# Decode block with its backward pass on one core: weight gradients and the x gradient as two background streams with buffers of their own

## The chip, the core and the metric

The kernel runs on one core of a Trainium2 chip. A core has a matrix engine (PE, with its weight loads PEld), a vector engine (DVE), a scalar engine (ACT), GpSimd (POOL) and SyncE (SP), each with its own in-order instruction queue. They work on SBUF tiles and on PSUM banks and wait for each other by semaphores. DMAs are issued from the queue of an engine and run beside it. The metric is the device time of one execution in microseconds, the median of several runs. A profiled execution gives the trace; its span is from the first to the last instruction.

## The reference, cut to what matters

One decode step (one position, batch 2) of a pre-norm block, and its vector-Jacobian product:

```python
B, Sq, D = 2, 1, 640;  Hq, Hkv, Sk, Dh = 32, 32, 4096, 128;  Dff = 1728
h   = x + attention(layernorm(x) @ wq, k_cache, v_cache) @ wo      # softmax over 4096 positions
out = h + relu(layernorm(h) @ w1) @ w2
_out, _vjp = jax.vjp(_f, A_x, A_k_cache, A_v_cache, A_wq, A_wo, B_w1, B_w2)
return (_out, *_vjp(grad_out))
```

The outputs are out_0 (the block's output), out_1 (gradient of x), out_2 and out_3 (gradients of the two caches, 2 x 32 x 4096 x 128 bf16, 67 MB each), and the weight gradients out_4 (wq, 640 x 4096), out_5 (wo, 4096 x 640), out_6 (w1) and out_7 (w2). With batch 2 each weight gradient is a product of rank 2: two rows of one vector set times two rows of another.

## The kernel before

**Two phases of 64 head turns.** Phase 1 (`p1_iter`, i = 0 to 65) takes one (batch, head) after the other: it loads the K and V tile (1 MB each), transposes K on PE, forms scores and softmax, and the products that later steps need. Phase 2 (`p2_iter`, j = 0 to 64) takes V again (tile W; 11 of the 64 are kept from phase 1), transposes it as pairs (`pair_transpose`, L366), gets `dp`, and writes two outer products on DVE, gK and gV (`outer_half`, L733, two halves each), which POOL stores to out_2 and out_3 (L773, L792). `plan` (L966) lays both side by side: phase 2 starts with i = 44 on every second turn, and from j = 11 it runs alone. A "turn" below is one such j. A turn without phase 1 is seven passes of the inner loop at L1060.

**The order is written by hand.** The program issues instructions in the order in which this Python code yields; no engine reorders its queue. Beside the turns, generators run in the background: `bg` (the middle layers; `go_group`, which gives the heads' output gradients goc and GQc; and last `mlp_out`, the product with w2 and out_0) and `bg2` (`fin_gen`, the weight gradients and the x gradient). `bg_step` gives each a credit per pass (its rate), and a generator pays what it yields; a yield of 0.0 means that it waits. `wait(n)` lets n counted steps go by (times `spread`, 2 when phase 2 runs alone), so that an instruction isn't put in the queue before its operand is likely to be there. After the last turn `forced` is set and what is left runs at once.

**Buffers.** Twelve equal homes ("big", 8 KB per partition) hold K, V, W, w2 and wq pieces, output tiles ot, and gK and gV. `take` and `give` hand them out from two lists, "ld" and "g"; `share(n)` moves homes to "g". `pump` issues the loads of `queue` on SP as "ld" homes come free; `reserve` (L1047) and `spare` (L1048) keep some back for `fin_gen` and `mlp_out`. A tile given back is handed out again in turn, and its new writer waits for the old reader or store.

**The weight gradients.** `rows_of` (L799) brings columns into row form: a copy on ACT (wide), four PE products into the PSUM bank "mid", a copy back. `outer_rows` (L818) forms an output group by group: up to three products of rank 2 into the banks mid, m and a, then three ACT copies to ot (L840), then a store from POOL's queue (L842). `gx_piece` (L856) loads one of six pieces of wq (wqs, L862), waits, transposes it on PE eight blocks at a time (L873, copies L875), and sums the products with GQc in bank m (L885), one add to gx1 per piece (L889). `fin_gen` runs out_7, out_6 (with a gx piece after each group), out_5 (the same), the rest of gx, the layer-norm backward and out_1 (`store_row`, L572, one buffer orow), and then out_4 with the rows of GQ. It is created when w1 is no longer needed (("w1", 1), L1049), in w1's place in SBUF.

**PSUM.** Eight banks: tps 2, sps 3, and m, a and mid one each.

Of the kernel before, what the change touches and what calls it, by code (L numbers as in the profile page):

```python
# [15 lines left out]
def kernel(  # L16
# [20 lines left out]
    nc = tc.nc  # L37
# [39 lines left out]
    homes = {"ld": list(range(NBIG)), "g": []}  # L77
    free = {"ld": NBIG, "g": 0}
    owned = {"ld": NBIG, "g": 0}
    stores = [0]  # L80
    spare = [2]
    home_of = {}

    def take(tag, shape, name):
        assert free[tag] > 0, (tag, name)
        free[tag] -= 1
        k = homes[tag].pop(0)
        t = big.tile(shape, BF16, tag=f"big{k}", bufs=1, name=name)
        home_of[id(t)] = (tag, k, t)
        return t  # L90

    def give(t, to=None):
        tag, k, _ = home_of.pop(id(t))
        to = to or tag
        owned[tag] -= 1
        owned[to] += 1
        free[to] += 1
        homes[to].append(k)

    def share(n):  # L100

        stores[0] = n
        while owned["g"] < n and free["ld"] > 0:
            homes["g"].append(homes["ld"].pop(0))
            for d in (free, owned):
                d["ld"] -= 1
                d["g"] += 1
# [464 lines left out]
    def store_row(col_bf, n, dst):  # L572
# [3 lines left out]
        r = small.tile([16, 128], BF16, tag="orow", bufs=1, name="orow")  # L576
# [49 lines left out]
    def mlp_out():  # L626
# [3 lines left out]
        for k in range(NW2):  # L630
            while free["ld"] < spare[0]:
                yield
            t = load_w2(k, "ld")
            yield from wait(8)
# [105 lines left out]
    def p2_iter(j, busy):  # L740
# [45 lines left out]
        give(c["W"], "g" if owned["g"] < stores[0] else "ld")  # L786
# [31 lines left out]
    def outer_rows(L, nrow, R, N, out_ap, cc, between=None):  # L818
# [5 lines left out]
        for c0 in range(0, cc, grp):  # L824
            gn = min(grp, cc - c0)
            while free["ld"] < spare[0]:
                yield
            ot = take("ld", [128, grp, N], "ot")
            todo = [(k, n0, min(512, N - n0)) for k in range(gn) for n0 in range(0, N, 512)]
            for t0 in range(0, len(todo), 3):  # L830
                part = []
                for k, n0, nn in todo[t0:t0 + 3]:
                    q = 32 * (fw[0] % 4)
                    o_ps = pst([128, 512], FP32, ("mid", "m", "a")[len(part)], "o_ps")
                    nc.tensor.matmul(o_ps[0:P, 0:nn], lhsT=L[q:q + B, bass.ds(c0 + k, P, step=cc)],
                                     rhs=R[q:q + B, n0:n0 + nn], start=True, stop=True)
                    part.append((o_ps, k, n0, nn))
                    fw[0] += 1
                for o_ps, k, n0, nn in part:
                    nc.scalar.copy(out=ot[0:P, k, n0:n0 + nn], in_=o_ps[0:P, 0:nn])  # L840
                yield 0.5 * len(part)
            nc.gpsimd.dma_start(out=out_v[:, c0:c0 + gn, :], in_=ot[0:P, 0:gn, :])  # L842
            give(ot)
            if between is not None:
                yield from between()

    def fin_gen(fin):
        gx1 = fin.tile([128, ND, B], FP32, tag="gx1", name="gx1")
        nc.vector.memset(gx1[:], 0.0)
# [3 lines left out]
        yield from wait(4)  # L853
        gx_next = [0]

        def gx_piece(k):  # L856

            hn = min(QP, H - k * QP)
            while free["ld"] < spare[0]:
                yield  # L860
            t = take("ld", [128, ND, QP * 128], "wqs")
            nc.sync.dma_start(out=t[:, :, 0:hn * 128], in_=wq_r[:, :, k * QP * 128:(k * QP + hn) * 128])  # L862
            yield from wait(6)
            todo = [(c, j) for j in range(hn) for c in range(ND)]
            acc = None
            prev = None
            for t0 in range(0, len(todo) + GT, GT):
                part = todo[t0:t0 + GT]
                nxt = None
                if part:  # L870
# [160 lines left out]
    for n, (i, j) in enumerate(plan):  # L1031
# [3 lines left out]
        if j == 0:  # L1035
            stores[0] = 3
# [87 lines left out]
```

## Time and profile before

| what | value |
|---|---|
| median of 6 runs | 1010.05 us (1005.01 to 1019.57) |
| the profiled execution | 1010.56 us; span 1008.8 us; mean granted TensorE clock 0.80 |
| busy in the span | PE 787.1, PEld 694.5, DVE 657.7, ACT 586.5, POOL 107.5 us |
| moved | 363.25 MB, mean 360 GB/s |
| ot copies (L840) | 160, the first at 698.9, the last at 1001.3 us |
| wqs transposes (L873) | 160, from 777.6 to 944.3 us |
| wqs issue to landing | 24.8 / 28.1 / 31.5 us (min, median, max) |
| ot issue to landing | 4.1 / 6.2 / 19.6 us |
| last gK store issued | 956.96 us |

A busy time is the sum of an engine's instruction times; it says nothing of where the engine was needed. The view by windows cuts it into stretches and gives the granted clock, the share of time in which the 16 DMA engines were busy, and the rate. The view of waits lists whose idle time was ended by whom. Phase 1 runs alone to about 330 us, with phase 2 to about 525 us; then phase 2 runs alone.

### The profile page before, as it was taken

The page shows a single profiled execution, that of the slowest core. Times are in us where ns is not written, and L with a number is a line of the kernel's source. Part 1 is how long each engine was busy: PE and PEld are TensorE (multiplying, and loading weights), DVE is VectorE, ACT ScalarE, POOL GpSimd, SP SyncE. Part 2 cuts the span into 40 slices and gives each one's busy share as a digit, 9 for nine tenths or more (in the row PEclk, how much of TensorE's full clock was granted, in tenths as well). Part 3 has the DMA queues.
Part 4 walks back from the last instruction along what each step waited for, and adds up shares of the span by engine and source line. Part 5 has one row for each costly group of instructions (what it writes and reads, how often), then busy time and mean ns, then how long its engine had stood idle before and what let it go on. Part 6 is the DMA issues. An engine that isn't in the chain of part 4 may idle for free.

```text
span 1008.8 us, 30245 instructions
## 1 busy us (share of the span) xinstructions
PE 787.1 (78%) x13169; PEld 694.5 (69%) x13173; DVE 657.7 (65%) x1289; ACT 586.5 (58%) x1261; POOL 107.5 (11%) x219
## 2 busy tenths in 40 slices
PE   6999999989899989999877746468485948764846
PEld 5988898989888888888866545356364836653611
DVE  3555767755387678787878888888673736663700
ACT  4666656667667767777644434245363727553747
POOL 0000000000000010000012121112211211211201
PEclk9999999999699989999995757576555658565655
DMA  9999999994577789999999999999799998999835
GB/s 350 416 401 384 355 378 407 363 386 172 208 255 284 301 314 377 423 422 421 401 353 425 423 371 425 407 426 413 306 379 412 364 420 333 422 424 417 329 128 208
DMA packets 63205, 363.25 MB, mean 360 GB/s; under 512 B 5696, under 2 KB 20928, under 8 KB 22880
## 3 DMA queue, kind: packets, MB, share of 16 engines
q1 hardware_dynamic: 42416, 212.18, 54.1%
q0 software_dynamic: 20656, 149.14, 35.7%
q8 instruction: 103, 1.69, 0.6%
q14 instruction: 30, 0.25, 0.1%
HBM read 212.16 MB, written 149.13 MB: 358 GB/s over the span
## 4 chain that ended last, share of the span: by engine, by line
PE 42%; DMA 29%; DVE 10%; issue 10%; ACT 7%; POOL 1%; SPq 0%; POOLq 0%; DVEq 0%; ACTq 0%
PE t_ps L353 10%; PE m_ps L408 10%; DMA wqs<-in_A_wq_dram 8%; DMA out_dram<-gK 8%; DMA out_dram<-gV 8%; DMA Kt<-in_A_k_cache_dram 6%; PE t_ps L374 5%; PE m_ps L423 4%; DVE gV L735 4%; ACT t_sb L358 4%; PE s_ps L364 4%; DVE gK L735 3%; PE dp_ps L387 1%; PE t_ps L345 1%; PE t_ps L873 1%
## 5 line engine op out<-in xcount | busy, mean ns | idle before, releaser
L358 ACT COPY t_sb<-t_ps 128x1024 bf16<-128x1024 bf16 x223 | 219.5, 1014 | 54.3 <-PE t_ps L353 52.1
L379 ACT COPY t_sb<-t_ps 128x512 f32<-128x512 f32 x256 | 148.7, 589 | 111.1 <-PE t_ps L374 107.7
L408 PE MATMUL m_ps<-pk,Vt 128*128 128x129 bf16 x2048 | 201.6, 226 | 5.9 <-issue 5.9
L374 PE MATMUL t_ps<-ident_f,Wt 128*128 128x128 f32 x848 | 181.5, 360 | 2.7 <-DMA Wt<-in_A_v_cache_dram 1.3
L415 DVE TENSOR_TENSOR pk<-Kt,ep 128x2048 bf16<-128x2048 bf16 x128 | 156.0, 1219 | 25.7 <-ACT ep L465 25.7
L735 DVE TENSOR_TENSOR gK<-rb,gsp 128x2048 bf16<-128x2048 bf16 x128 | 152.2, 1228 | 31.6 <-DMA out_dram<-gV 18.1
L735 DVE TENSOR_TENSOR gV<-rb,pp 128x2048 bf16<-128x2048 bf16 x128 | 152.3, 1218 | 23.4 <-DMA out_dram<-gK 11.0
L353 PE MATMUL t_ps<-ident_bf,Kt 128*128 128x128 bf16 x2048 | 155.6, 227 | 4.5 <-issue 2.4
L408 PEld LDWEIGHTS <-Vt 128*128 128x128 bf16 x2048 | 133.4, 102 | 15.3 <-issue 10.0
L374 PEld LDWEIGHTS t_ps<-ident_f,Wt 128*128 128x128 f32 x848 | 129.1, 186 | 16.8 <-issue 6.4
L353 PEld LDWEIGHTS <-Kt 128*128 128x128 bf16 x2048 | 129.1, 102 | 8.5 <-issue 4.1
L387 PEld LDWEIGHTS <-t_sb 128*128 128x128 bf16 x2048 | 90.7, 104 | 51.0 <-ACT t_sb L379 41.1
L387 PE MATMUL dp_ps<-gom,t_sb 128*128 128x2 bf16 x2048 | 93.9, 167 | 23.7 <-ACT t_sb L379 22.6
L364 PE MATMUL s_ps<-qc,t_sb 128*128 128x1 bf16 x2048 | 89.1, 164 | 13.2 <-ACT t_sb L358 8.6
L364 PEld LDWEIGHTS <-t_sb 128*128 128x128 bf16 x2048 | 79.8, 97 | 18.2 <-ACT t_sb L358 12.8
L840 ACT CAST ot<-o_ps 128x512 bf16<-128x512 f32 (+4 forms) x160 | 65.9, 491 | 22.4 <-DMA out_dram<-ot 13.2
L792 POOL DMA_DIRECT2D out_dram<-gV x64 | 34.2, 534 | 393.1 <-DVE gV L735 288.0
L356 DVE COPY t_sb<-t_ps 128x1024 bf16<-128x1024 bf16 x33 | 22.8, 692 | 66.3 <-PE t_ps L353 66.3
L518 ACT ACTIVATE MT<-m_ps,rtot 128x128 bf16<-128x128 f32 x64 | 23.6, 368 | 70.0 <-PE m_ps L408 65.8
L423 PE MATMUL m_ps<-ep,Kt 128*128 128x1 bf16 x2048 | 61.0, 163 | 1.8 <-ACT OU L519 1.2
L773 POOL DMA_DIRECT2D out_dram<-gK x64 | 34.0, 531 | 256.6 <-DVE gK L735 221.4
L423 PEld LDWEIGHTS <-Kt 128*128 128x128 bf16 x2048 | 58.6, 96 | 2.1 <-issue 1.7
(186 smaller groups left out, 872.8 us busy)
## 6 DMA issues: line engine op xcount, KB each, us to landing
Kt<-in_A_k_cache_dram SPq DMA_DIRECT2D x64, 1024.0 KB, 9.6
Vt<-in_A_v_cache_dram SPq DMA_DIRECT2D x64, 1024.0 KB, 8.5
out_dram<-gV POOLq DMA_DIRECT2D x64, 1024.0 KB, 11.2
out_dram<-gK POOLq DMA_DIRECT2D x64, 1024.0 KB, 10.8
Wt<-in_A_v_cache_dram SPq DMA_DIRECT2D x53, 1024.0 KB, 10.7
wo_t<-in_A_wo_dram SPq DMA_DIRECT2D x4, 1280.0 KB, 11.0
out_dram<-ot POOLq DMA_DIRECT2D x5, 1024.0 KB, 4.1
wq_t<-in_A_wq_dram SPq DMA_DIRECT2D x5, 960.0 KB, 10.0
```

Source lines behind the costliest of these rows:

```text
L353: nc.tensor.transpose(t_ps[:, j, :], nat[:, g * GT + j, :], ident_bf[:])
L358: nc.scalar.copy(out=t_sb[:], in_=t_ps[:])
L364: nc.tensor.matmul(dst[:, sc:sc + 1], lhsT=t_sb[:, j, :], rhs=vec, start=True, stop=True)
L374: nc.tensor.transpose(t_ps[:, j, :], natf[:, 2 * cc:2 * cc + 2, :].rearrange("p c k -> p (c k)"), ident_f[:])
L379: nc.scalar.copy(out=t_sb[:], in_=t_ps[:])
L387: nc.tensor.matmul(dst[:, sc:sc + 2], lhsT=v[:, j, :, par], rhs=vecs[:, par, :], start=(par == 0), stop=(par == 1))
L408: nc.tensor.matmul(r["m"][:, 0:129], lhsT=r["V"][:, sc, :], rhs=r["pk"][sc // HALF][:, sc % HALF, 0:129], start=False, stop=(sc == NSC - 1))
L415: nc.vector.tensor_tensor(out=p["pk"][k][:, :, 0:128].rearrange("p s (a two) -> p s a two", two=2), in0=p["K"][:, sl, :].rearrange("p s (a ...
L423: nc.tensor.matmul(r["m"][:, 129:130], lhsT=r["K"][:, sc, :], rhs=r["ep"][:, sc, 0:1], start=(sc == 0), stop=False)
L735: nc.vector.tensor_tensor(out=pairs_view(dst[:, sl, :]), in0=row.rearrange("p (a two) -> p a two", two=2)[:, None, :, :].to_broadcast([128 ...
L792: nc.gpsimd.dma_start(out=natural(out_3, b, h), in_=gV[:])
L840: nc.scalar.copy(out=ot[0:P, k, n0:n0 + nn], in_=o_ps[0:P, 0:nn])
```

## The change

It does the following.

- Homes come in four lists: "ld", "g", "f" (tiles of the weight gradients) and "q" (w2 and wq pieces). `share` takes a wanted number for each list, and a home that is given back goes to a list that lacks one. From turn 36 the wanted numbers are ld 4, g 4, f 3, q 2; when both background streams have ended, ld 7 and g 6. `reserve` and `spare` are gone.
- A thirteenth home, `big2`, is made in w1's place beside the pool fin and goes to "f".
- `fin_gen` forms the weight gradients alone: out_7, out_6, out_5, out_4, the last two in halves of 16 heads. `gx_gen` is a third background list, `bg3`, with a rate of its own (0.45; bg2's is 0.65, it was 0.85).
- `outer_rows` puts its products in the banks m and a in turn, each followed one step later by the copy of the one before; a home rests 13 steps before it is used again (`rested`). Once all of goc is there (`late`), every third copy is on DVE. The stores are issued from ACT's queue.
- `gx_gen` fetches wq pieces as soon as all of goc is there and a "q" home is free, two at a time at most, and starts a piece 20 steps after its fetch. Its products go by column blocks to bank mid, with an add on DVE for each group of eight.
- `mlp_out` takes its w2 pieces from "q" and waits 12 steps instead of 8. `store_row` has two orow buffers.
- Steps are counted in `bg_step(1, ...)`. During phase 1 bg2 gets no credit. What is left at the end runs in rounds over bg, bg3 and bg2.

```diff
-    homes = {"ld": list(range(NBIG)), "g": []}
-    free = {"ld": NBIG, "g": 0}
-    owned = {"ld": NBIG, "g": 0}
-    stores = [0]
-    spare = [2]
+    homes = {"ld": list(range(NBIG)), "g": [], "f": [], "q": []}
+    free = {tag: len(v) for tag, v in homes.items()}
+    owned = dict(free)
+    wanted = {}
+    pools = [big] * NBIG
     home_of = {}
+    given_at = {}
     def take(tag, shape, name):
         assert free[tag] > 0, (tag, name)
         free[tag] -= 1
         k = homes[tag].pop(0)
-        t = big.tile(shape, BF16, tag=f"big{k}", bufs=1, name=name)
+        t = pools[k].tile(shape, BF16, tag=f"big{k}", bufs=1, name=name)
         home_of[id(t)] = (tag, k, t)
...
+    def goes_to(tag):
+
+        if owned[tag] > wanted.get(tag, NBIG):
+            for other in homes:
+                if owned[other] < wanted.get(other, 0):
+                    return other
+        return tag
+
     def give(t, to=None):
         tag, k, _ = home_of.pop(id(t))
-        to = to or tag
+        to = to or goes_to(tag)
         owned[tag] -= 1
         owned[to] += 1
         free[to] += 1
         homes[to].append(k)
-
-    def share(n):
-
-        stores[0] = n
-        while owned["g"] < n and free["ld"] > 0:
-            homes["g"].append(homes["ld"].pop(0))
-            for d in (free, owned):
-                d["ld"] -= 1
-                d["g"] += 1
+        given_at[k] = step[0]
+
+    def rested(tag, n):
+
+        return free[tag] > 0 and (forced[0] or step[0] >= given_at.get(homes[tag][0], -n) + n)
+
+    def share(**want):
+
+        wanted.clear()
+        wanted.update(want)
+        for tag in homes:
+            while free[tag] > 0 and goes_to(tag) != tag:
+                to = goes_to(tag)
+                homes[to].append(homes[tag].pop(0))
+                for d in (free, owned):
+                    d[tag] -= 1
+                    d[to] += 1
+
+    def more_home(tag, pool):
+        homes[tag].append(len(pools))
+        pools.append(pool)
+        free[tag] += 1
+        owned[tag] += 1
...
-        r = small.tile([16, 128], BF16, tag="orow", bufs=1, name="orow")
+        r = small.tile([16, 128], BF16, tag="orow", bufs=2, name="orow")
...
-            while free["ld"] < spare[0]:
+            while free["q"] < 1:
                 yield
-            t = load_w2(k, "ld")
-            yield from wait(8)
+            t = load_w2(k, "q")
+            yield from wait(12)
...
-        give(c["W"], "g" if owned["g"] < stores[0] else "ld")
+        give(c["W"], "g" if j < H and owned["g"] < 3 else None)
...
-    def outer_rows(L, nrow, R, N, out_ap, cc, between=None):
+    late = [False]
+
+    def outer_rows(L, nrow, R, N, out_ap, cc):
         P = nrow // cc
...
         out_v = out_ap.rearrange("(p c) n -> p c n", c=cc)
         for c0 in range(0, cc, grp):
             gn = min(grp, cc - c0)
-            while free["ld"] < spare[0]:
-                yield
-            ot = take("ld", [128, grp, N], "ot")
+            while not rested("f", 13):
+                yield 0.0
+            ot = take("f", [128, grp, N], "ot")
             todo = [(k, n0, min(512, N - n0)) for k in range(gn) for n0 in range(0, N, 512)]
-            for t0 in range(0, len(todo), 3):
-                part = []
-                for k, n0, nn in todo[t0:t0 + 3]:
+            made = []
+            for x in range(len(todo) + 1):
+                if x < len(todo):
+                    k, n0, nn = todo[x]
                     q = 32 * (fw[0] % 4)
-                    o_ps = pst([128, 512], FP32, ("mid", "m", "a")[len(part)], "o_ps")
+                    o_ps = pst([128, 512], FP32, "ma"[fw[0] % 2], "o_ps")
+                    fw[0] += 1
                     nc.tensor.matmul(o_ps[0:P, 0:nn], lhsT=L[q:q + B, bass.ds(c0 + k, P, step=cc)],
                                      rhs=R[q:q + B, n0:n0 + nn], start=True, stop=True)
-                    part.append((o_ps, k, n0, nn))
-                    fw[0] += 1
-                for o_ps, k, n0, nn in part:
-                    nc.scalar.copy(out=ot[0:P, k, n0:n0 + nn], in_=o_ps[0:P, 0:nn])
-                yield 0.5 * len(part)
-            nc.gpsimd.dma_start(out=out_v[:, c0:c0 + gn, :], in_=ot[0:P, 0:gn, :])
+                    made.append((o_ps, k, n0, nn))
+                    yield 0.3
+                if x > 0:
+                    o_ps, k, n0, nn = made[x - 1]
+                    if late[0] and x % 3 == 0 and x < len(todo):
+                        nc.vector.tensor_copy(out=ot[0:P, k, n0:n0 + nn], in_=o_ps[0:P, 0:nn])
+                    else:
+                        nc.scalar.copy(out=ot[0:P, k, n0:n0 + nn], in_=o_ps[0:P, 0:nn])
+                    yield 0.3
+            nc.scalar.dma_start(out=out_v[:, c0:c0 + gn, :], in_=ot[0:P, 0:gn, :])
             give(ot)
-            if between is not None:
-                yield from between()
     def fin_gen(fin):
-        gx1 = fin.tile([128, ND, B], FP32, tag="gx1", name="gx1")
-        nc.vector.memset(gx1[:], 0.0)
         FIN["wide"] = [fin.tile([128, 4, 4, 32], BF16, tag="wide", bufs=2, name="wide") for _ in range(2)]
         for w in FIN["wide"]:
             nc.vector.memset(w[:], 0.0)
-        yield from wait(4)
-        gx_next = [0]
-
-        def gx_piece(k):
-
+        yield from wait(2)
...
+        yield from outer_rows(FIN["ar"], Dff, FIN["gr"], D, out_7, Dff // 96)
+        yield from rows_of(fin, ghfc, NF, "ghfr", "rX")
+        yield from rows_of(fin, x2c, ND, "x2r", "rD")
+        yield from outer_rows(FIN["x2r"], D, FIN["ghfr"], Dff, out_6, ND)
+        HH = H // 2
+        while ("gh1", B - 1) not in done:
+            yield
+        yield from rows_of(fin, gh1c, ND, "gh1r", "rD")
+        for s0 in range(0, H, HH):
+            yield from rows_of(fin, OFc[:, s0:s0 + HH, :], HH, "OFr", "rX")
+            yield from outer_rows(FIN["OFr"], HH * 128, FIN["gh1r"], D, out_5[s0 * 128:(s0 + HH) * 128, :], HH)
+        yield from rows_of(fin, x1c, ND, "x1r", "rD")
+        for s0 in range(0, H, HH):
+            while not all(("go", B - 1, h) in done for h in range(s0, s0 + HH)):
+                yield
+            yield from rows_of(fin, GQc[:, s0:s0 + HH, :], HH, "GQr", "rX")
+            yield from outer_rows(FIN["x1r"], D, FIN["GQr"], HH * 128, out_4[:, s0 * 128:(s0 + HH) * 128], ND)
+
+    def gx_gen(fin):
+        gx1 = fin.tile([128, ND, B], FP32, tag="gx1", name="gx1")
+        nc.vector.memset(gx1[:], 0.0)
+        tiles = []
+
+        def fetch():
+            while len(tiles) < NQ and free["q"] > 0:
+                k = len(tiles)
+                hn = min(QP, H - k * QP)
+                t = take("q", [128, ND, QP * 128], "wqs")
+                nc.sync.dma_start(out=t[:, :, 0:hn * 128], in_=wq_r[:, :, k * QP * 128:(k * QP + hn) * 128])
+                tiles.append((t, step[0]))
+
+        while not all(("go", B - 1, h) in done for h in range(H)):
+            yield 0.0
+        for k in range(NQ):
+            while k >= len(tiles) or (step[0] < tiles[k][1] + 20 and not forced[0]):
+                fetch()
+                yield 0.0
+            t = tiles[k][0]
             hn = min(QP, H - k * QP)
-            while free["ld"] < spare[0]:
-                yield
-            t = take("ld", [128, ND, QP * 128], "wqs")
-            nc.sync.dma_start(out=t[:, :, 0:hn * 128], in_=wq_r[:, :, k * QP * 128:(k * QP + hn) * 128])
-            yield from wait(6)
-            todo = [(c, j) for j in range(hn) for c in range(ND)]
-            acc = None
+            todo = [(c, j) for c in range(ND) for j in range(hn)]
             prev = None
             for t0 in range(0, len(todo) + GT, GT):
                 part = todo[t0:t0 + GT]
...
                     nxt = (t_sb, part)
                     if t0 + GT >= len(todo):
                         give(t)
+                        fetch()
                     yield 0.9
                 if prev is not None:
-                    if acc is None:
-                        acc = pst([128, ND, B], FP32, "m", "gx_ps")
+                    acc = pst([128, ND, B], FP32, "mid", "gx_ps")
+                    c0, c1 = prev[1][0][0], prev[1][-1][0] + 1
                     for x, (c, j) in enumerate(prev[1]):
-
                         nc.tensor.matmul(acc[:, c, :], lhsT=prev[0][:, x, :], rhs=GQc[:, k * QP + j, :],
-                                         start=(c == 0 and j == 0), stop=(c == ND - 1 and j == hn - 1))
+                                         start=(x == 0 or prev[1][x - 1][0] != c),
+                                         stop=(x == len(prev[1]) - 1 or prev[1][x + 1][0] != c))
+                    nc.vector.tensor_tensor(out=gx1[:, c0:c1, :], in0=gx1[:, c0:c1, :], in1=acc[:, c0:c1, :], op=ALU.add)
                     yield
                 prev = nxt
-            nc.vector.tensor_tensor(out=gx1[:], in0=gx1[:], in1=acc[:], op=ALU.add)
-
-        def gx_ready():
-
-            k = gx_next[0]
-            if k < NQ and all(("go", B - 1, h) in done for h in range(k * QP, min(H, (k + 1) * QP))):
-                gx_next[0] += 1
-                yield from gx_piece(k)
-
-        yield from rows_of(fin, acol, NF, "ar", "rF")
-        yield from rows_of(fin, gc, ND, "gr", "rD")
-        yield from outer_rows(FIN["ar"], Dff, FIN["gr"], D, out_7, Dff // 96)
-        yield from rows_of(fin, ghfc, NF, "ghfr", "rF")
-        yield from rows_of(fin, x2c, ND, "x2r", "rD")
-        yield from outer_rows(FIN["x2r"], D, FIN["ghfr"], Dff, out_6, ND, gx_ready)
-        while ("gh1", B - 1) not in done:
-            yield
-        yield from rows_of(fin, OFc, H, "OFr", "rH")
-        yield from rows_of(fin, gh1c, ND, "gh1r", "rD")
-        yield from outer_rows(FIN["OFr"], HD, FIN["gh1r"], D, out_5, HD // 128, gx_ready)
-        while gx_next[0] < NQ:
-            yield from gx_ready()
-            yield
...
+            yield from wait(2)
...
-        yield from rows_of(fin, GQc, H, "GQr", "rH")
-        yield from rows_of(fin, x1c, ND, "x1r", "rD")
-        yield from outer_rows(FIN["x1r"], D, FIN["GQr"], HD, out_4, ND)
...
-        q = (bg, bg2)[k]
+        step[0] += int(k == 1)
+        q = (bg, bg2, bg3)[k]
         credit[k] = min(credit[k] + rate, 2.0) if q else 0.0
         while q and credit[k] > 0.0:
...
-    RATE2 = 0.85
+    RATE2 = 0.65
+    RATE3 = 0.45
...
-        if j == 0:
-            stores[0] = 3
         if i is None and plan[n - 1][0] is not None:
-            share(4)
-        if j == H + KEPT[1]:
-            share(5)
+            share(ld=KEPT[1] + 3, g=4)
+        if fin is not None and not bg2 and not bg3:
+            share(ld=7, g=6)
+        elif fin is not None and j >= H + KEPT[1] - 1:
+            share(ld=4, g=4, f=3, q=2)
         if j is not None:
             while g2 is not None:
                 p2_step()
             if j < NP1:
                 bg_until(("go", *turns[j]))
...
-        reserve[0] = 2 if bg2 and j is not None and j >= H + 4 else 0
-        spare[0] = 1 if j is not None and j >= H + 2 else 2
         if i is None and ("w1", 1) in done and fin is None:
             wts.release()
             fin = tc.alloc_tile_pool(name="fin", bufs=1)
+            big2 = tc.alloc_tile_pool(name="big2", bufs=1)
+            more_home("f", big2)
             bg2.append(("fin", fin_gen(fin)))
+            bg3.append(("gx", gx_gen(fin)))
+        late[0] = all(("go", B - 1, h) in done for h in range(H))
...
+                bg_step(2, RATE3)
...
     forced[0] = True
     slot[0] = 99
-    while bg2:
-        bg_one(bg2)
+    left = [q for q in (bg, bg3, bg2) if q]
+    while left:
+        for q in left:
+            bg_one(q)
+        left = [q for q in left if q]
+    big2.release()
```

More of the change, by code (lines that the diff above doesn't have):

```diff
@@ new lines, in fin_gen @@
+        yield from rows_of(fin, acol, NF, "ar", "rX")
+        yield from rows_of(fin, gc, ND, "gr", "rD")
+        yield from outer_rows(FIN["ar"], Dff, FIN["gr"], D, out_7, Dff // 96)
[6 more added lines that the diff above has]
+        yield from rows_of(fin, gh1c, ND, "gh1r", "rD")
@@ L918, in fin_gen @@
             nc.vector.tensor_copy(out=gxo[:], in_=gx_bf[:, :, b])
+            yield from wait(2)
             store_row(gxo[:], ND, out_1[b].rearrange("s (c p) -> (s c) p", p=128))
             yield
-        yield from rows_of(fin, GQc, H, "GQr", "rH")
-        yield from rows_of(fin, x1c, ND, "x1r", "rD")
-        yield from outer_rows(FIN["x1r"], D, FIN["GQr"], HD, out_4, ND)
     bg = []
     bg2 = []
+    bg3 = []
     done = set()
-    credit = [0.0, 0.0]
+    credit = [0.0, 0.0, 0.0]
     def bg_one(q):
@@ L945, in bg_step @@
     def bg_step(k, rate):
-        step[0] += k
-        q = (bg, bg2)[k]
+        step[0] += int(k == 1)
+        q = (bg, bg2, bg3)[k]
         credit[k] = min(credit[k] + rate, 2.0) if q else 0.0
@@ L995 @@
     queue.insert(0, ("wq", 0))
-    reserve = [0]
     def pump():
@@ L1004, in pump @@
                 tag = "ld"
-                if free["ld"] <= reserve[0]:
+                if free["ld"] < 1:
                     return
@@ L1017 @@
     pump()
-    fin = None
+    fin = big2 = None
     g2 = None
@@ L1084 @@
             bg_step(0, rate)
-            bg_step(1, RATE2)
+            bg_step(1, 0.0)
         if i is not None and i in (H + 1, NP1 + 1):
```

## The prediction, made before the run

> **What bounds the kernel now.** I read the page's slices first, then the busy time and DMA rate by stage, then the same view over the places where the rate drops, then the waits, then the timeline of the end.
>
> ```profile
> PEclk9999999999699989999995757576555658565655
> DMA  9999999994577789999999999999799998999835
> HBM read 212.16 MB, written 149.13 MB: 358 GB/s over the span
> ```
>
> By stage, a line's fields are the window, its length, busy time (instructions) of PE, PEld, DVE, ACT and POOL, then granted clock, DMA share and GB/s:
>
> ```profile
> 525.00:592.00 67.00, 39.80 (x501) 35.05 (x502) 55.92 (x94) 24.85 (x47) 12.73 (x26) 0.64 1.01 419
> 592.00:710.00 118.00, 73.18 (x861) 61.98 (x860) 103.59 (x172) 50.58 (x106) 22.50 (x46) 0.66 1.00 407
> 710.00:745.00 35.00, 21.91 (x197) 17.59 (x196) 24.19 (x41) 18.03 (x46) 7.27 (x15) 0.50 0.84 316
> 745.00:955.00 210.00, 145.07 (x1672) 118.57 (x1671) 118.22 (x140) 113.37 (x232) 39.49 (x76) 0.63 0.97 395
> 955.00:1008.80 53.80, 29.09 (x94) 9.33 (x93) 3.81 (x16) 31.98 (x76) 4.78 (x9) 0.50 0.40 163
> ...
> 720.00:730.00 10.00, 8.23 (x66) 5.88 (x66) 5.24 (x9) 7.66 (x20) 1.05 (x2) 0.50 0.52 201
> 780.00:790.00 10.00, 9.76 (x125) 7.87 (x122) 6.23 (x9) 7.95 (x16) 1.58 (x3) 0.67 0.76 272
> 835.00:845.00 10.00, 9.38 (x137) 8.19 (x135) 8.21 (x11) 8.49 (x16) 2.26 (x4) 0.73 0.65 214
> 935.00:940.00 5.00, 4.46 (x49) 4.03 (x49) 3.84 (x5) 2.98 (x8) 1.83 (x4) 0.50 0.56 226
> ```
>
> From 525 us on the transfers set the pace: 419 GB/s, share 1.01, no engine full but DVE. The rate fails in three kinds of place: around 720, in short holes between 780 and 940, and from 955 to the end, where 53.8 us move 163 GB/s.
>
> The waits (who, for whom: us in total, times, longest):
>
> ```profile
> PE t_ps L873 <- DMA wqs<-in_A_wq_dram: 45.9, 4, 17.8
> DVE orow L577 <- DMA out_dram<-orow: 21.6, 2, 17.5
> PE o_ps L835 <- ACT ot L840: 18.7, 12, 13.6
> ACT ot L840 <- DMA out_dram<-ot: 13.2, 1, 13.2
> ```
>
> The timeline of POOL at the end, with the idle time before each issue in brackets:
>
> ```profile
> 985.50 0.53 POOL L842 DMA_DIRECT2D out_dram<-ot  x1 [24.43 <-ACT ot L840]
> 989.70 0.53 POOL L842 DMA_DIRECT2D out_dram<-ot  x1 [3.66 <-ACT ot L840]
> 1002.27 0.53 POOL L842 DMA_DIRECT2D out_dram<-ot  x1 [3.66 <-ACT ot L840]
> ```
>
> Each hole follows one engine standing in order: ACT 13.2 us at 707 (a store tile given out again before its store had landed), PE 11.8 us at 766 and again until 920 (the wq piece not landed), DVE 17.5 us at 819 (one orow buffer). During each stall the DMA stays full from its backlog; the hole comes afterwards. In the end stretch nothing overlaps: the last gK leaves at 957.0, then x gradient, rows of GQ and all of out_4 in a row.
>
> **The change, part by part.** The sum stands against the profiled run: span 1008.8, run 1010.56 us; the median, 1010.05, lies 0.5 lower. Bytes are unchanged. From 525 they are 178.9 MB (rates times windows, in 25 us steps); the full rate is taken as 421 GB/s, as most full 5 us windows read 419 to 429.
>
> Here a rule speaks against any gain. The windows above hold 419 over 67 us. The Trainium skill, "DMA: Bandwidth & Descriptors", Specifications, gives about 358 GB/s as the HBM limit of a core and says that side binds HBM-to-SBUF traffic. By it 361.3 MB need 1009 us, exactly the span, and overlapping the end could win nothing. By the row, 421 is held for long stretches and 358 is only a mean over full and empty ones. I follow the row.
>
> 1. *The end (out_4 and x gradient into the streams).* 53.8 us x 163 GB/s = 8.77 MB, at 421 20.8 us: 33.0 us go. A last transfer stays: an ot store lands 6.2 us after issue (median), 2.5 of that being 1 MB at 421, so 4 us come back. This needs the streams to finish in time. A turn without phase 1 makes seven background steps. The f stream adds 0.65 per step; rows cost 1.7 per four columns, a part 0.6, and with one home a tile rests 13 steps. Counted through all six row/product blocks that is about 270 steps, 38 turns. It can begin at turn 21 (w1 done at 590, gV20 issued at 589.5), so it ends near turn 60 of 64. The gx stream begins when all of goc is there (743, turn 40); a piece costs 5.6 at 0.45, or the 20-step age, about 16 steps: six pieces, some 95 steps, to turn 54. The three w2 pieces can be held off by gx's immediate refetch of both q homes; then 3 x 24 steps plus little, to turn 62 or 63. Cover: the turns themselves. If w2 misses it, some 10 us return.
>
> 2. *ot's reuse (rest of 13 steps, three f homes).* The hole 720-730 is worth 10 x (1 - 201/421) = 5.2 us. It goes. The rest of 710-745 (8.7 in all) I leave, since four freed W homes now pass to f and q in turn.
>
> 3. *Earlier wq, 20 steps of age, two homes; orow bufs 2.* Holes at 780, 835 and 935: 3.5 + 4.9 + 2.3 = 10.7 us go if the stalls before them go.
>
> Gross: 33.0 - 4 + 5.2 + 10.7 = 44.9.
>
> 4. *What it adds.* Matmuls, row matmuls (112), transposes (160) and copies (160) stay the same in number. Stores rise from 17 to 18 and move from POOL to ACT. The trace shows no ACT issue; unblocked SP issues take 0.33 to 0.70 us, so 18 x 0.38 = 7 us of ACT (bounds 0 and 12.6), with t_sb and rb copies queued behind, for which PE waits. ACT is 54% busy in 745-955: nothing on the path. POOL loses L842's waits, so gK and gV stores never stand behind ACT. SP keeps the same wqs and w2 issues, in order among W loads that wait for freed homes.
>
> PE gets new waits. The gx sums now go to DVE in 21 adds instead of 6 (15 x 0.162 = 2.4 us of DVE), each holding the single mid bank until DVE has passed its outer products, 2.36 us a pair; rows, w2 sums and the next gx group queue behind it on PE. A late copy on DVE (every third part from turn 40 on: 16 of out_5, 10 of out_4) holds m or a likewise. With half a pair each, and 0.4 for the copy, 15 x 1.2 + 26 x 1.6 = 60 us of PE order; bounds 0 and twice that. How much of a PE stall reaches the DMA? In the trace some 80 us (45.9 + 18.7 + 17.5) left 15.9 us of holes, a fifth. So 12 us (0 to 24).
>
> Last, does a wq piece land in 20 steps? A turn of 7.5 to 8.7 us makes that 21 to 25 us; the six rows read 24.8 to 31.5, median 28.1, with W running up to four ahead. Now W has four homes, three ahead: 28.1 x 4/5 = 22.5, no stall. Against it: the same page, Queues, rings and completion order, says each DMA engine goes round-robin over the queue rows with work. The trace has one row of loads and one of stores; ot on ACT makes a third, so loads fall from a half to a third while an ot store is in flight: 34 us, 11 short, six times 66 us of PE, a fifth is 13 us. Eighteen stores of 6 to 10 us fill some 40% of 340 us, so I take 4 us.
>
> Sum: 44.9 - 12 - 4 = 28.9; span 980, time 981.7, against the median 981.
>
> **Rivals.**
> *A, the DMA runs full to the end.* 525 + 178.9/0.421 + 4 = 954, time 956. For: 420 was held even while PE stood. Against: three streams now meet in the same turns.
> *C, the gain is given back as a PE bound.* At the half clock (0.50 in most rows) a turn's own work is 16 W transposes x 0.27 + their products and rb 2.2 = 6.5 us; over turns 36 to 60 that is 156 us, and parts 43, gx 25.5, rows 13 come on it: 238 us, 9.9 a turn, over the DMA's 8.7. With a quarter of step 4's waits unhidden, 253. Then 710 + 9 (out_7 and part of out_6, 3.7 MB, moved ahead of it) + 253 + 4 turns x 7.4 + 8 = 1010 with the last landing, time 1012. Against: at 840-860 PE is dense, its clock 0.93 to 1.0, and a transpose takes 0.16.
> *D, slower.* The mid bank: PE cold as in C, and every one of the 21 adds finds DVE at the start of a pair: 238 + 21 x 2.4 = 288 us, time 1046. It decides from 24 us of such waits unhidden on a cold PE (10.9 us a turn). For: PE waited up to 1.4 us for a gx add already. Against: DVE was idle over 40% of 745-955.
> *E, the early start fails.* If the home in w1's place serves nothing before turn 38, when the first W home has been handed over and has rested, 26 turns x 7 x 0.65 = 118 of the 140 units of rows and parts are done; 22, or 37 parts at 0.5 us, stand at the end: 18 us, time 995.
>
> **How the numbers follow.** Likeliest (981, own range 966 to 996) 0.50; A 0.20; C 0.11; D 0.13; E 0.06, half of it within 1%. A measurement of this kernel can tell about 1% from no change. Faster 0.20 + 0.50 + 0.03 = 0.73; within 1% 0.11 + 0.03 = 0.14; slower 0.13. The range 954 to 1014 leaves out D and the edge of A.
>
> **What would show it.** Right: ot copies from about 605 instead of 698.9; 400 GB/s or more until within 15 us of the end; no GQ rows after the last gK; no orow wait; the stall at wqs under 5 us each; turns 40 to 60 of 8.7 to 9.3 us. Wrong: PE full at clock 0.5 with DMA under 0.9; PE or DVE waits on mid's adds above 40 us; a last gK after 985; w2 or out_0 after it.

## The result, and the profile after

The changed kernel takes 1000.11 us (median of 33 runs, 992.26 to 1014.44), the kernel before 1009.85 us in the same comparison (70 runs): ratio 0.991, 95% interval 0.9892 to 0.9928. (The ratio leaves out runs that are over 1.5% slower than the fastest of their kernel, so it is not quite that of the medians.) The gain is real, and a third of the 29 us that were forecast. The profiled execution has a span of 1000.9 us at a mean granted clock of 0.777 (before 1008.8 us, 0.800).

The page, slices of 25.0 us:

```profile
PEclk9999998999799989999996756555655555655657
DMA  9999999995577789999999999998998999998878
HBM read 212.16 MB, written 149.13 MB: 361 GB/s over the span
```

The two poor slices at the end are now 7 and 8 instead of 3 and 5, and slice 29 (700 us) is a 9 instead of a 7; in exchange slices at 675, 750 and 900 us have fallen from 9 to 8. The view by windows says where (window, length, busy us and instructions of PE, PEld, DVE, ACT, POOL, granted clock, DMA share, GB/s):

```profile
525.00:592.00 67.00, 38.50 (x486) 33.89 (x485) 56.20 (x97) 24.77 (x47) 13.35 (x26) 0.64 1.01 423
592.00:710.00 118.00, 85.82 (x761) 68.28 (x761) 89.99 (x150) 57.34 (x131) 18.73 (x41) 0.53 0.95 372
710.00:745.00 35.00, 27.36 (x269) 21.20 (x268) 28.74 (x46) 20.14 (x44) 7.27 (x15) 0.60 0.98 393
745.00:955.00 210.00, 166.50 (x1541) 123.11 (x1539) 116.18 (x169) 112.82 (x231) 28.30 (x59) 0.54 0.93 366
955.00:1000.90 45.90, 23.41 (x267) 18.12 (x266) 29.24 (x39) 15.84 (x30) 9.10 (x17) 0.69 0.85 343
```

Read as time lost against the 421 GB/s of the prediction, length x (1 - rate / 421):

| stretch | before | after | best version (below) |
|---|---|---|---|
| 592-710 | 3.9 us | 13.7 us | 8.7 us |
| 710-745 | 8.7 | 2.3 | 2.2 |
| 745-955 | 13.0 | 27.4 | 7.0 |
| 955 to the end | 33.0 | 8.5 | 4.9 |
| sum | 58.6 | 52.0 | 22.8 |

The end and the stretch around the hole at 720 gained 31 us, nearly the forecast (33.0 - 4 + 5.2 = 34). The two long stretches in the middle lost 24 us more than before, while PE was busy for 73% and 79% of them. The waits from 592 to 970 us (who, for whom: us in total, times, longest; "issue" is standing that no wait explains):

```profile
DVE gx L945 <- PE gx_ps L942: 48.1, 20, 5.7
PE o_ps L862 <- ACT ot L871: 47.0, 56, 2.7
PEld L862 <- issue: 35.2, 52, 3.0
PEld t_ps L397 <- issue: 28.9, 32, 2.0
PE rw_ps L833 <- DVE gom L304: 10.1, 1, 10.1
```

The waits of before for orow and for wqs are not in this list (PE waits 0.3 us for orow, and no longer for wqs). In their place PE, about to make a product of rank 2 (o_ps, L862), stands 56 times for the ACT copy out of the bank that it needs (L871). The timeline at 630 us shows how (start, duration, engine, line, operation, idle time before it in brackets):

```profile
630.16 0.26 PEld L862 LDWEIGHTS <-ar 2*96 2x96 bf16 x3 [0.33 <-issue]
630.16 0.76 PE L862 MATMUL o_ps<-gr,ar 2*96 2x512 bf16 x2
...
630.95 0.75 ACT L871 CAST ot<-o_ps 96x512 bf16<-96x512 f32 x2
...
631.59 0.58 PE L862 MATMUL o_ps<-gr,ar 2*96 2x512 bf16 x2 [0.67 <-ACT ot L871]
631.59 0.41 PEld L862 LDWEIGHTS <-ar 2*96 2x96 bf16 x2 [1.17 <-issue]
...
632.20 0.75 ACT L871 CAST ot<-o_ps 96x512 bf16<-96x512 f32 x2 [0.50 <-PE o_ps L862]
632.83 0.58 PE L862 MATMUL o_ps<-gr,ar 2*96 2x512 bf16 x1 [0.67 <-ACT ot L871]
633.34 0.71 PEld L397 LDWEIGHTS t_ps<-ident_f,Wt 128*128 128x128 f32 x4 [1.34 <-issue]
```

PE and ACT take turns: two products, then ACT copies, PE stands 0.67 us, then two more. Behind PE stand the transposes of W (L397), which the next gK and gV need. In the new loop product x goes into the bank of product x-2, and the order is product x, copy of x-1, product x+1; product x+1 needs the bank of x-1, whose copy was issued just ahead of it. The "step" between them is only a yield of 0.3: with a credit of 0.65, one pass of the inner loop issues two or three such pieces together, and then nothing of the turn lies between the copy and the product that waits for it (PE has only these products from 630.16 to 633.34).

The end, in POOL's timeline:

```profile
989.83 0.53 POOL L815 DMA_DIRECT2D out_dram<-gV  x1 [2.32 <-DVE gsp L771]
992.42 0.53 POOL L796 DMA_DIRECT2D out_dram<-gK  x1 [2.06 <-DVE gK L758]
```

The last gK is issued 8.5 us before the end of the span; before it was 51.8 us. The turns themselves have become long: from turn 36 (gV issued at 724.9) to turn 59 (969.0) they take 244.1 / 23 = 10.6 us each, and the last four, with the streams done, 5.2 us.

### The profile page after: what moved, and what is told of

Its sections match the earlier page's. It is cut to its first block, busy times and chain, and to the rows that moved or that the text cites. A ratio compares the mean times of both kernels' runs of the same rounds, so it can differ in the third digit from the quotient of the medians.

```text
span 1000.9 us, 30166 instructions
## 1 busy us (share of the span) xinstructions
PE 818.3 (82%) x13169; PEld 716.2 (72%) x13173; DVE 673.3 (67%) x1328; ACT 578.1 (58%) x1238; POOL 97.5 (10%) x202
## 4 chain that ended last, share of the span: by engine, by line
PE 58%; DMA 14%; ACT 14%; DVE 8%; issue 5%; POOL 0%; ACTq 0%; SPq 0%; POOLq 0%; DVEq 0%
PE t_ps L397 13%; PE t_ps L376 10%; PE m_ps L431 10%; DMA out_dram<-gV 6%; PE o_ps L862 5%; PE m_ps L446 4%; ACT t_sb L381 4%; PE s_ps L387 4%; DMA Kt<-in_A_k_cache_dram 3%; DVE gV L758 3%; ACT t_sb L402 3%; PE dp_ps L410 3%; ACT ot L871 3%; DMA out_dram<-gK 3%; DVE gK L758 2%
## 5 line engine op out<-in xcount | busy, mean ns | idle before, releaser
L397 PE MATMUL t_ps<-ident_f,Wt 128*128 128x128 f32 x848 | 197.2, 382 | 2.5 <-DMA Wt<-in_A_v_cache_dram 1.5
L397 PEld LDWEIGHTS t_ps<-ident_f,Wt 128*128 128x128 f32 x848 | 138.6, 198 | 39.2 <-issue 30.6
L410 PEld LDWEIGHTS <-t_sb 128*128 128x128 bf16 x2048 | 96.0, 107 | 49.2 <-ACT t_sb L402 25.4
L387 PEld LDWEIGHTS <-t_sb 128*128 128x128 bf16 x2048 | 79.8, 97 | 20.1 <-ACT t_sb L381 13.4
L871 ACT CAST ot<-o_ps 128x512 bf16<-128x512 f32 (+4 forms) x137 | 60.8, 477 | 12.3 <-PE o_ps L862 8.0
L379 DVE COPY t_sb<-t_ps 128x1024 bf16<-128x1024 bf16 x33 | 22.8, 692 | 66.5 <-PE t_ps L376 66.5
L446 PEld LDWEIGHTS <-Kt 128*128 128x128 bf16 x2048 | 58.6, 96 | 2.4 <-issue 2.0
```

Source lines behind the costliest of these rows:

```text
L387: nc.tensor.matmul(dst[:, sc:sc + 1], lhsT=t_sb[:, j, :], rhs=vec, start=True, stop=True)
L397: nc.tensor.transpose(t_ps[:, j, :], natf[:, 2 * cc:2 * cc + 2, :].rearrange("p c k -> p (c k)"), ident_f[:])
L410: nc.tensor.matmul(dst[:, sc:sc + 2], lhsT=v[:, j, :, par], rhs=vecs[:, par, :], start=(par == 0), stop=(par == 1))
L446: nc.tensor.matmul(r["m"][:, 129:130], lhsT=r["K"][:, sc, :], rhs=r["ep"][:, sc, 0:1], start=(sc == 0), stop=False)
```

## The experiments

Ratios are to the kernel before, with 95% intervals; the changed kernel's is 0.991 (0.9892 to 0.9928). "ot waits" are PE's waits for the copies to ot from 592 to 970 us, 51.8 us in 62 in the changed kernel (47.0 for ACT, 4.8 for DVE); "issue gaps" are all the standing of PE and PEld under "issue" there, 121 us. The two overlap, since PEld often stands while PE waits. Differences in us are between medians taken beside different runs of the kernel before; by the ratios they can be 3 or 4 us smaller.

**Do the products on 32-row blocks cost something by themselves?** The products stay as they are, one at a time, but contract over all 128 rows, of which all but two are zero. (The ACT copy that spreads the columns becomes smaller too.)

```diff
-  nc.scalar.copy(out=w[:, 0:cn, :, 0:B], in_=col[:, c0:c0 + cn, None, :].to_broadcast([128, cn, 4, B]))
+  nc.scalar.copy(out=w[:, 0:cn, 0, 0:B], in_=col[:, c0:c0 + cn, :])
-  lhsT=L[q:q + B, ...], rhs=R[q:q + B, n0:n0 + nn]
+  lhsT=L[:, ...],       rhs=R[:, n0:n0 + nn]
```

> Each rank-2 product reads all 128 rows (the other rows are zero; one copy of the two vectors in the row form in place of four) instead of a block of rows at 32q. Copies, banks, pace and stores stay. Theory M (PE order: each product on a row block, standing alone between full-height work, empties the array before and after it, 0.33 and 0.44 us, which is most of the 119 us that PE's weight loads stand with nothing named): those gaps fall below 40 us, turns 43 to 59 shorten from 11.6 to 10 us or less, time 965 to 985. Theory B (two banks: product waits for copy, 52 us): gaps may go but PE waits for ot stay near 50 us, time 995 to 1003. Theory D (DVE standing for the gx sums and for late copies): no change, 997 to 1003.

Measured 988.97 us, 0.9826 (0.9787 to 0.9866). The ot waits stayed (53.6 us); the issue gaps fell to 97 us, and the mean clock rose to 0.815. So without the row blocks the kernel is 11 us faster here (8 by the ratios), and the ot waits do not come from them.

**The old loop in the new kernel.** Products in threes (mid, m, a), then three copies, one step for all; all else as changed.

```diff
+  for t0 in range(0, len(todo), 3):
+      part = []
+      for k, n0, nn in todo[t0:t0 + 3]:
+          o_ps = pst([128, 512], FP32, ("mid", "m", "a")[len(part)], "o_ps")
...
+      for o_ps, k, n0, nn in part: ...   # the copies
+      yield 0.6 * len(part)
```

> Products in threes again, in the banks mid, m and a, with the three copies behind them in the same step; same pace (0.6 per part), same streams, homes and stores, every third copy on DVE when late. Theory M: one gap for three products, 60 groups in place of 160: time 975 to 990. Theory B: the waits for ot fall by half or more and the time with them, 975 to 990. Theory D: 998 to 1006, since mid is now shared with the gx sums.

Measured 975.51 us, 0.9698 (0.9628 to 0.9768): 25 us faster than the change. The ot waits are 4.8 us in 6. With this loop the change comes in below its forecast of 981, so the missing gain lay here. In place of the ot waits the old stall for wqs is back, at half its former size (45.9 us before):

```profile
PE t_ps L927 <- DMA wqs<-in_A_wq_dram: 24.3, 3, 13.6
```

**The DVE copies and the sums of gx, where the prediction had put PE's new waits.** In the first, `late[0] = False`: no copy goes to DVE. In the second, the add to gx1 is made only for the last of the 22 groups, so out_1 lacks most of the x gradient.

> All 160 copies of the products on ACT, none on DVE. Theory D: DVE's 16.4 us of waits for products go, stores leave sooner, time 985 to 993. Theories M and B: PE order keeps its length, time 997 to 1006.

> Of the 22 adds of gx sums on DVE only the last is kept, so gx1 lacks the other groups: out_1 is not the whole x gradient. The products on PE stay. Theory D (DVE stands 48 us for these sums and its outer products start late): time 975 to 990. Theories M and B: 995 to 1002.

Measured 1001.26 us, 0.993 (0.9893 to 0.9967), and 997.14 us, 0.9884 (0.9859 to 0.9908), with ot waits of 52.2 and 49.0 us. Neither can be told from the change (the second's median is 3 us lower, its interval overlaps). The 48.1 us for which DVE stands for gx_ps cost next to nothing: DVE was busy for only 55% of 745-955.

**Which part of the old loop helps: three row blocks at work together, the third bank, or the order?** Three kernels. The first keeps the threes but puts all of a group on the same 32 rows. The second makes pairs, in m and a alone. The third puts the change's loop (single products, m and a in turn, copy behind the next product) into the kernel before.

```diff
-  q = 32 * (fw[0] % 4)          # threes, one block
+  q = 32 * (t0 // 3 % 4)
...
-  for t0 in range(0, len(todo), 3):      # pairs
+  for t0 in range(0, len(todo), 2):
-  ("mid", "m", "a")[len(part)]
+  "ma"[len(part)]
```

> As e2_threes, but the three products of a group use one and the same block of rows (32q) instead of three different ones; the block changes from group to group. Banks, copies and pace as in e2. Theory M2 (three products on different row blocks run at once: three took 0.65 us in e2, a single one 0.58 to 0.64 in the changed kernel): three take 1.2 to 1.9 us, time 983 to 992. Theory B (what counts is the third bank and the grouped copies): 973 to 979.

> As e2_threes, but products in pairs on two different row blocks, in the banks m and a, the two copies behind them. Theory M2: two for the price of one: between the changed kernel and e2, 980 to 988. Theory B (a third bank is needed): 993 to 1002. If only the emptying of the array counts (80 groups in place of 160 or 54): 977 to 985.

> The kernel before with nothing changed but the product loop: one product at a time, banks m and a in turn, each copy after the next product, pace 0.5 per product as before, stores on POOL. Theory M2: 120 products in the middle lose their company, 80 more PE slots of 0.6 to 1 us, of which the transfers hide a part: 1017 to 1035. If singles cost nothing by themselves and only hurt where three streams meet: 1006 to 1013.

Measured: one block 975.0 us, 0.9644 (0.9583 to 0.9706); pairs 976.78 us, 0.9635 (0.9548 to 0.9721), ot waits 13.6 us in 18. Both are as good as the threes, so it is neither the blocks nor the third bank. In the pairs, too, no other product lies between the copy out of a bank and the next product into it; what lies there is other PE work of the turns (pairs at 810.50 and 811.69 us, with transposes of W and products with gom between them). The change's loop in the kernel before gives 1033.11 us, 1.0212 (1.0158 to 1.0266), and brings the same wait with it, from 592 to 985 us (before, 18.7 us in 12 over the whole span, 13.6 of them in one):

```profile
PE o_ps L837 <- ACT ot L843: 44.3, 57, 8.8
```

**The copy moved by one place.** Single products, m and a in turn, one part each, as in the change; the copy is issued with its own product, and 27 instead of 23 copies fall to DVE. In words:

```diff
-  product x;  yield 0.3;  copy of x-1;  yield 0.3
+  product x;  copy of x;  yield 0.6
```

> The changed kernel with one line moved: products one at a time in the banks m and a in turn, but each copy is issued with its own product, not one step later behind the next product; 0.6 per part in one piece. Theory W (the late copy: PE's next product stands for a bank that is emptied only behind the copy issued just ahead of it, 52 us): those waits fall below 15 us, time 975 to 983. Theory G (160 separate entries of a row-block product into the full-height work, a gap ahead and behind each): gaps stay near 120 us, time 990 to 1000. Both in part: 983 to 990.

Measured 970.99 us, 0.9642 (0.9571 to 0.9713), span 968.8, against 1007.18 us of the kernel before beside it: the fastest median of all (though the intervals of the threes, the pairs and the other kernels without the change's order overlap its own), 29 us under the change (27 by the ratios). Its timeline shows PE at the next transposes while ACT copies:

```profile
829.84 0.64 PE L859 MATMUL o_ps<-gh1r,OFr 2*128 2x512 bf16 x1
830.41 1.11 PE L397 MATMUL t_ps<-ident_f,Wt 128*128 128x128 f32 x4
830.52 0.58 ACT L864 CAST ot<-o_ps 128x512 bf16<-128x512 f32 x1
```

Its windows and waits:

```profile
592.00:710.00 118.00, 91.88 (x854) 72.56 (x852) 93.39 (x153) 64.25 (x143) 20.53 (x44) 0.57 0.99 390
745.00:955.00 210.00, 179.78 (x1699) 136.85 (x1698) 132.29 (x193) 123.18 (x242) 33.49 (x67) 0.54 1.00 407
955.00:968.80 13.80, 0.37 (x8) 0.29 (x8) 4.82 (x5) 0.08 (x1) 1.52 (x3) 0.50 0.66 272
```

```profile
PE o_ps L859 <- ACT ot L864: 12.2, 16, 3.0
PEld L859 <- issue: 17.8, 32, 3.3
PEld t_ps L397 <- issue: 9.1, 15, 1.7
```

At the same granted clock (0.54) PE does 10% more instructions in 745-955 than in the changed kernel and the DMA share is 1.00. The ot waits (15.1 us with DVE's) fell by 36.7, the issue gaps to 73 us, the time by 29.

**Is it the lateness of the copy, or the distance from it to the bank's next use?** Here the copy still comes a step after its product, but the loop issues it ahead of the next product, which then uses the other bank. In words:

```diff
-  product x;      yield 0.3;  copy of x-1;  yield 0.3
+  copy of x-1;    yield 0.3;  product x;    yield 0.3
```

> The changed kernel with the two halves of the loop body exchanged: each step issues the copy of the product before, then the next product. A copy is as late behind its own product as in the change, but the next product that needs its bank comes a whole part later. Theory W (what counts is the distance from a copy to the next product on the same bank): 971 to 981. If the lateness of a copy behind its product is what costs: 994 to 1004.

Measured 979.67 us, 0.9688 (0.9629 to 0.9747), ot waits 20.2 us in 29 (16.9 for ACT). A late copy with a product between it and the bank's next user is nearly as good: it is the distance. And in the kernel before, single products with the copy at once:

> The kernel before with products one at a time in the banks m and a, each copy issued with its own product (e7 had the copy behind the next product and took 1033). Theory W: the loss of e7 goes, 1003 to 1015. If single products in themselves cost PE order there: 1025 to 1035.

Measured 1021.37 us, 1.0133 (1.0066 to 1.02): outside the 1003 to 1015 that were expected. It is 12 us better than the change's loop there (8 by the ratios, whose intervals overlap). By the profiled runs, one of each, the last gK leaves at 956.96 us in the kernel before, 973.70 with the change's loop, 960.05 with the copy moved; so in these traces the loop costs 16.7 us in the overlapped part, and the order of the copy is 13.7 of them. From the last gK to the last copy to ot it is 44.3, 50.3 and 50.3 us: in the bare tail, where no work of the turns is left to lie between, single products in two banks cost 6 us against threes in three, in either order. There POOL's stores of eight products follow each other by 4.2 us with the threes and by 5.0 us with both loops of single products.

**Side questions.** On top of the threes: stores of ot from POOL's queue instead of ACT's; an age of 28 steps instead of 20 for a wq piece; the weight gradients started at turn 36 instead of 21. On top of the copy at once: full rows, as in the first experiment.

> As e2_threes, with the 18 stores of the products issued from POOL as before the change. If a third row of transfers costs loads their share (the prediction's 4 us): 968 to 974. If POOL's stores of gK and gV then stand behind ACT again: 977 to 985. If neither: within 3 us of e2's 975.5.

> e2_threes with 28 steps instead of 20 between the fetch of a wq piece and its first use. PE stood 24.3 us in three places for wq pieces in e2. If those stalls reach the transfers by a fifth, as the prediction took it: 970 to 973. If they are covered: 973 to 979. If the gx stream then ends after the turns: over 980.

> e2_threes, but the weight gradients begin at turn 36 instead of turn 21 (the thirteenth home stays unused until then; the homes of turn 36 are the same). The prediction's step 1 holds that turns 21 to 36 carry three tiles of out_7 and one of out_6 at the price of their bytes. If so, some 22 parts or more stand behind the last turn: 985 to 1000. If the streams had room to spare at turn 60: 973 to 980.

> e8 with the products over all 128 rows as in e1 (no gaps, copies at once, one at a time). Theory W: the same as e8 within 4 us. Theory G: 10 to 15 us below e8. Both in part: 5 to 10 us below e8.

Measured: POOL stores 980.8 us, 0.9691 (0.9638 to 0.9745), the ratio of the threes; age 28 gives 973.26 us, 0.9651 (0.9588 to 0.9713); the late start 980.17 us, 0.9713 (0.9653 to 0.9772). None of the three can be told from the threes (0.9698). With the late start 592-710 runs at 416 GB/s and 710-745 at 335, against 388 and 414 with the early start: what the early start costs in the first stretch it saves in the second and after it (745-955: 406 GB/s against 393). Full rows give 975.26 us, 0.9664 (0.9604 to 0.9724), at a mean clock of 0.851 against 0.775: no faster than without. The gain of the first experiment is there only while PE sets the pace.

## Why the prediction was partly right, and its gain three times too high

**Right: what went.** The end stretch: 33.0 us lost were expected to become 4, and became 8.5; the weight gradients ended in turn 59 (counted: near 60), their copies began at 607 us (605). The store tile's hole (5.2 us) went, the 710-745 stretch as a whole lost 6.4 us less. The waits for orow and wqs went; by itself this brought nothing to 745-955, because another wait took their place. For wqs it was in part luck: at 10.6 us a turn the age of 20 steps lasts 30 us, and with the DMA at 0.93 a piece landed in 11.4 us (median). With the DMA full, in the threes and with the copy at once, it took 18.7 and 19.7 us, near the 22.5 assumed, and PE waited again, 24.3 and 7.5 us. The 358 GB/s that the prediction quotes is no limit here, as it had read from the row: 423 over 67 us.

**The step that failed is step 4, in two places: what the new order costs PE, and how much of it reaches the time.** It let matmuls and copies "stay the same in number" and so costed the new order in `outer_rows` at nothing. Yet the change's fourth point said it: products in two banks in turn, "each followed one step later by the copy of the one before". Writing out four products in issue order would have shown that product x+1 stands behind the copy of x-1, issued just before it, and 160 products of this kind were there to be multiplied by the wait for one ACT copy. The prediction looked for new PE waits at DVE instead (60 us at mid's adds and the late copies). Measured: 4.8 us for the late copies and 0.3 for mid's adds, as the two kernels without them confirm, but 47.0 us for ACT. The size of PE's waiting (60 us expected, 51.8 measured) was nearly hit by luck; the mechanism was another one.

**And the fifth.** The share of a PE stall that reaches the DMA was taken from the kernel before, where PE had slack and the transfers a backlog. In the changed kernel PE's order was the bound in the middle: taking away 36.7 us of ot waits brought 29 us, four fifths and not one fifth. The threes, the one block, the pairs and the exchanged halves took away 32 to 47 us and brought 20 to 25, half to two thirds, with the DMA full again from 745 to 955 us (share 1.00 or 1.01) and new waits for wqs (7 to 24 us) in all four. These shares lump the waits with the issue gaps, which fell beside them. With 0.5 to 0.8 in place of 0.2 the measured 52 us are 26 to 41, and the forecast's own line becomes 44.9 - 26 - 4 = 15 down to 44.9 - 41 - 4, about 0. The measured 9 us lie between.

**The rivals.** Rival C had the right bound for the middle: 9.9 us a turn for PE's work at the half clock, 10.5 with its waits, measured 10.6 (the likeliest case had 8.7 to 9.3). It put its waits at the wrong engine, and its time (1012) is 12 too high; the last turns were 5.2 us, not 7.4. D's waits at mid were not there. E didn't happen, and a start at turn 36 costs nothing that the runs show; its 995 is also some 5 us less than its own 18 us on top of 981.7, with no reason given. A was not reached by any kernel.

**Also wrong.** 592-710 was counted as untouched and lost 9.8 us more than before: the same waits, and once 10.1 us at 686-696 for PE behind a DVE operation (gom) before rows could be formed. The 4 us for a third row of transfers do not show: with the DMA full, wqs landed in 18.7 us (median) with the stores on ACT's queue and in 20.7 with them on POOL's, at the same ratio. The adds of gx are 22, not 21. gx and w2 came in another order than assumed (gx to turn 57 instead of 54, w2 not held off), without harm. Once the copy is moved, the kernel is at 971 us, 10 below the forecast of 981: the terms of the sum other than the order in `outer_rows` were, if anything, too cautious.

**Open.** Why full rows gain in the changed kernel stays open: the issue gaps fell by 24 us, but the granted clock in 745-955 rose as well, from 0.54 to 0.64, and no run separates the two. That the row-block products empty the array around them, as an expectation has it, no trace shows. Whether moving the copy and keeping a third bank would give more was not tried.

## What to carry to other kernels

When products rotate through PSUM banks, write down the issue order of a few of them and, for each bank, what PE has to do between the copy out of it and the next product into it. Count this in passes of the whole program, not in yields of one generator: several yields can go out together. With two banks, and each copy issued behind the next product and just ahead of the one after, it was often nothing (29 us of 1000 here, mended by moving one line); one product, or the work of a turn between pairs in the same two banks, was nearly enough (14 to 20 us of waits left of 52). Count waits by the engine that the new order makes wait, not by the buffers that look scarce; and take the share of a stall that reaches the end from the regime after the change: where PE was the bound it was half to four fifths, where it had slack a fifth.

## What was unexpected in the hardware

- Around a single product on a 32-row block among full-height work the weight loads stand: PEld 0.33 us ahead of the first one (630.16 us), and 0.43 to 0.44 us behind a lone one, while it runs, ahead of the next transposes. Three in a row take about as long as one (0.65 us against 0.58 to 0.64). While PE set the pace, full rows were worth 8 to 11 us; when it did not, nothing.
- With the copy at once, full rows instead of row blocks raise the granted clock in 745-955 from 0.54 to 0.76, with PE busy for 67% instead of 86% and as many instructions (1704 against 1699). The higher clock is no gain by itself: over the span 0.851 (975.26 us) against 0.775 (970.99 us), with the DMA share at 1.00 in that stretch in both.
- In the changed kernel and the best version PE was busy for 79 and 86% of 745-955 at a mean granted clock of 0.54: a densely used PE stayed near half speed through that stretch.
- A store issued from ACT's queue took ACT 0.32 to 0.39 us, 18 of them, and none was seen to delay the end.
